# Chunk choice for both head groups at once, two blocks in halves, and loads reordered, in a fused attention and feed-forward kernel

## The chip, the cores and the metric

The kernel runs on one core of one Trainium2 chip. The metric is the device time of one execution in microseconds (us), as a median over runs. The engines are named as in the profile: PE is TensorE (matmuls), PEld its weight loads, DVE is VectorE, ACT is ScalarE, POOL is GpSimd and SP is SyncE, which here only starts DMAs. Every instruction of the profile carries the kernel line that issued it, such as L834.

## The reference

Two parts follow one another. The first is attention with a choice of key chunks: 4 batches, 8 heads, 768 tokens, 64 dimensions, keys in chunks of 32.

```python
k_min, k_max = min and max of k over each chunk of 32 keys
ub = sum_d(max(q * k_min, q * k_max))           # one bound for each query and chunk
ub = where(chunk is not in the future, ub, -1e9)
sel = the 6 chunks of highest ub for each query
scores = where(sel & causal, q @ k.T / 8, -1e9)
attn_out = softmax(scores) @ v
```

The second takes the result as 3072 tokens of width 512, normalizes by the root mean square (times `rms_g`), and computes `(silu(x @ w_gate) * (x @ w_val)) @ w_out` with an inner width of 1536. Inputs and output are float32; inside the kernel most tensors are bf16.

## The kernel before

The work is cut into 12 blocks of 256 tokens (4 batches, 3 blocks m = 0, 1, 2 of each). `ORDER` lists them; blocks 0 to 3 of the order are the first blocks (m = 0) of the four batches. Each block has two head groups of four heads, and each pair of block and group is one call of `job`. Within it:

- `turn` transposes k and q on DVE (L525), `half` makes bf16 copies (L532, L533), `ext0` and `ext1` take minimum and maximum of each chunk (L540), and `dk`, `bd0`, `bd1` put them into the matrix BD (L545, L552).
- `upper` (L587) multiplies q and its positive part with BD on PE: 32 small matmuls, the bounds of all chunks. For m = 0 only the last 64 columns of each head pair need them, since earlier tokens have at most six chunks.
- `ubn` (L597) transposes the bounds on DVE, `bar` (L604) sets the future chunk to a large negative value, `top` (L611) finds the eight largest, `mk` (L616) compares with the sixth, `mt` (L620) and `swap` (L627 on DVE or L631, L632 on ACT) turn the mask for use on PE as mtd and mto.
- `scores` (L657, and L668 for the mask) goes into the PSUM buffers S, `exp` (L707, ACT) into pt, the triangle (L677, POOL) clears the future, `values` (L733, PE) multiplies with v, and `rden` and `norm` (L748, L752) divide.

`norm` turns a block's tokens into xsT (L768 to L809, with PE transposes L796). `ffn` runs the gate and value matmuls wg and wv (L834, called gates here) into the PSUM buffers F, tanh (L841, ACT), tg (L845, DVE), a copy vs (L853, ACT) and the product hh (L856, POOL), or, where `DIRECT` says so, the product on DVE straight from PSUM (L849). `project` (L866) multiplies hh with wo, `out` copies (L880, L882), and SP stores (L886).

Block 0 is in `SPLIT`: its tokens go in two halves of 128, its first half needs no mask, and its gates have 128 moving columns instead of 256. A gate step of 512 columns (two or four of wo's 128 rows) needs one third of wg and wv: the weights come in three DMAs each, wg, wv in turns and then wo, all issued by POOL. The inputs are issued by SP and, for block 0, by ACT.

Nothing is ordered by hand: `Plan` simulates the engines with assumed durations, gives each operation a priority, and writes out the order in which the engines get their instructions. `pool` holds numbered buffers; pools named in `in_order`, hh among them, are given out strictly in the order of the program. `due_attn` and `due_ffn` place a block's attention 70 us ahead of its feed-forward part. Where PE would idle before 60 us, the planner puts in matmuls of the identity with itself (`keep_busy`, L921): filler that computes nothing that is used. `HELD` makes the loads of two blocks wait for a weight:

```python
HELD = {2: (("wv", 2), ("wo", 1)), 3: (("wo", 1), ("wo", 2))}   # block: (before k and q, before v)
```

S has 2 buffers (a scores step takes both, an upper step one), F has 4, hh 13, pt 6.

Of the kernel before, what the change touches and what calls it, by code (L numbers as in the profile page):

```python
# [8 lines left out]
FP32 = mybir.dt.float32  # L9
# [8 lines left out]
NEG = -1.0e30  # L18
# [3 lines left out]
class Op:  # L22
# [3 lines left out]
    def __init__(self, name, eng, occ, lat, fn, pri):  # L26
        self.name, self.eng, self.occ, self.lat, self.fn, self.pri = name, eng, occ, lat, fn, pri
        self.deps, self.takes, self.uses, self.users, self.after = [], [], [], [], []
        self.dma = None
        self.slack = 0.0  # L30
        self.mode = None
        self.done = None
        self.alts = {eng: (occ, lat, fn)}


class Rings:

# [6 lines left out]
    def _step(self, until):  # L44
        while True:
            heads = [q[0] for q in self.queue.values() if q]
            nxt = self.wait[0][0] if self.wait else None
            if not heads:
                if nxt is None or nxt > until:
                    return  # L50
                self.now = max(self.now, nxt)
            else:
                cycle = sum(d[1] for d in heads)
                end = self.now + min(d[0] for d in heads) * cycle
                stop = min(end, until, nxt if nxt is not None else end)
                if stop > self.now:
                    for d in heads:
                        d[0] -= (stop - self.now) / cycle
                    self.now = stop
                for q in self.queue.values():  # L60
                    if q and q[0][0] <= 1e-9:
                        q[0][2](self.now)
                        q.pop(0)
            while self.wait and self.wait[0][0] <= self.now + 1e-12:
                _, ring, d = self.wait.pop(0)
                self.queue.setdefault(ring, []).append(d)
            if self.now >= until and not (self.wait and self.wait[0][0] <= until):
                if not any(q and q[0][0] <= 1e-9 for q in self.queue.values()):
                    return

    def add(self, t, ring, packets, cost, op):
        self._step(min(t, self.wait[0][0]) if self.wait else t)

        def landed(now, op=op):
            op.done = now + (0.9 if op.dma[2] else 1.2) + op.slack
        op.done = None
        self.wait.append((t, ring, [packets, cost, landed]))
        self.wait.sort(key=lambda w: w[0])
        self.guess()
# [28 lines left out]
class Plan:  # L108
# [4 lines left out]
    PATIENT = {}  # L113
# [38 lines left out]
    def run(self, in_order=(), fill=None):  # L152
# [25 lines left out]
        def est(o, e):  # L178
# [6 lines left out]
            for key in o.takes:  # L185
                p = self.pool_of[key]
                need[p] = need.get(p, 0) + 1
                if p in strict and self.fifo[p][head[p]] is not o:
                    return None
# [18 lines left out]
        while todo:  # L208
# [58 lines left out]
            for key in o.takes:  # L267
                p = self.pool_of[key]
                if p in strict:
                    head[p] += 1  # L270
                self.free[p].sort()
                slot[key] = self.free[p].pop(0)[1]
# [16 lines left out]
def kernel(  # L289
# [37 lines left out]
    def buffers(name, n, shape, dtype, space=sb):  # L327
        store[name] = [space.tile(shape, dtype, name=f"{name}{i}") for i in range(n)]
        plan.pool(name, n)
# [13 lines left out]
    buffers("ubn", 2, [P, 2, 4, CH], FP32)  # L343
    buffers("m8", 2, [P, 2, 4, 8], FP32)
    buffers("mk", 2, [P, 2, 4, CH], BF16)
    buffers("mtd", 5, [P, 2, 4, CH], BF16)
    buffers("mto", 5, [P, 4, CH], BF16)
# [34 lines left out]
    PACE, LEAD = 23.0, 70.0  # L382
    MARGIN = 3.0
    FIRST = 8
    SPLIT = {0}
    PACKED = {0, 1, 2}
    DIRECT = {(i, hp) for i in range(len(ORDER)) for hp in range(KH) if i >= 6 and hp % 2}
# [67 lines left out]
    HELD = {2: (("wv", 2), ("wo", 1)), 3: (("wo", 1), ("wo", 2))}  # L455

    def load_qk(i, nm, src):
# [3 lines left out]
        for n, a in enumerate((0, 2, 1, 3)):  # L461
            eng = ("SP", "ACT")[n % 2] if i == 0 else "SP"
            rows = slice(32 * a, 32 * (a + 1))
            if i in PACKED:
                sv = src[b].rearrange("(g a) (m r j) d -> a m r g (j d)", a=4, m=NBLK, r=32)[a, m]
                todo = [(sv, lambda rows=rows: at(key)[rows].rearrange("r g j h d -> r g (j h d)"),
                         4, 0.098)]
# [14 lines left out]
    def loads_due(i, n):  # L482
        return -500 + 10 * i + n if i < 2 else due_attn(i) - 30 + n

    def load_v(i):
        b, m = ORDER[i]
        key = ("vraw", b, m)
        for e in range(2):
# [3 lines left out]
                64, 0.02, loads_due(i, 2 if i != 1 else -1), writes=[key],  # L492
# [14 lines left out]


    def job(i, g):
# [67 lines left out]
        ub, ubn, m8, mk = ("ub", *J), ("ubn", *J), ("m8", *J), ("mk", *J)  # L577
        mtd, mto = ("mtd", *J), ("mto", *J)

        def upper():  # L580
            qs = [at(qT)[:, :, BLK - w:], qr()]
            qs = [x.rearrange("p h (j c r) -> p h j c r", c=2, r=CH) for x in qs]
            o, d = at(ub), BD[b, g]
            for t in range(4):
                for hp in range(2):
                    for c in range(2):
                        TE.matmul(o[64 * c:64 * (c + 1), hp, 0:32 * nj],  # L587
                                  d[64 * hp:64 * (hp + 1), t, :],
                                  qs[t // 2][64 * hp:64 * (hp + 1), t % 2, :, c, :],
                                  start=(t == 0), stop=(t == 3))  # L590

        o = plan.op(f"upper{J}", "PE", 0.925 if m else 0.49, 1.09 if m else 0.66, upper, base + 3,
                    reads=[bd] + [bd + (x,) for x in range(m + 1)] + [qT, qR, qraw], writes=[ub],
                    takes=[(ub, "S")])
        o.mode = "sq"
        j0 = 4 - nj
        plan.op(f"ubn{J}", "DVE", 0.37 if m else 0.17, 0.445 if m else 0.25, lambda: VE.transpose(  # L597
            out=at(ubn).rearrange("p h j c -> p h (j c)")[:, :, 0:32 * nj],
            in_=at(ub)[:, :, 0:32 * nj]), base + 3, reads=[ub], writes=[ubn], takes=[(ubn, "ubn")])

        def bar():
            f = at(ubn)[0:64].rearrange("p h j c -> p h (j c)")
            c = CB * m + 2 * j0 + 1
            VE.memset(f[:, :, c:c + 34 * (nj - 1) + 1:34], NEG)  # L604

        plan.op(f"bar{J}", "DVE", 0.09, 0.12, bar, base + 3, reads=[ubn], writes=[ubn])

        def top():
            for h in range(2):
                for j in range(nj):  # L610
                    VE.max(out=at(m8)[:, h, j, :],  # L611
                           in_=at(ubn)[:, h, j, 0:CB * m + 2 * (j0 + j) + 2])

        plan.op(f"top{J}", "DVE", 0.083 * 2 * nj, 0.083 * 2 * nj + 0.08, top, base + 3,
                reads=[ubn], writes=[m8], takes=[(m8, "m8")])
        plan.op(f"mk{J}", "DVE", 0.35 if m else 0.15, 0.42 if m else 0.22, lambda: VE.tensor_tensor(  # L616
            out=at(mk)[:, :, 0:nj], in0=at(ubn)[:, :, 0:nj],
            in1=at(m8)[:, :, 0:nj, TOPK - 1:TOPK].to_broadcast([P, 2, nj, CH]), op=ALU.is_lt),
            base + 3, reads=[ubn, m8], writes=[mk], takes=[(mk, "mk")])
        plan.op(f"mt{J}", "DVE", 0.37 if m else 0.17, 0.445 if m else 0.245, lambda: VE.transpose(  # L620
            out=at(mtd).rearrange("p h j c -> p h (j c)")[:, :, 0:32 * nj],
            in_=at(mk).rearrange("p h j c -> p h (j c)")[:, :, 0:32 * nj]),
            base + 3, reads=[mk], writes=[mtd], takes=[(mtd, "mtd")])

        def swap():
            for r, c, h in ((slice(0, 64), slice(64, 128), 0), (slice(64, 128), slice(0, 64), 1)):
                VE.transpose(out=at(mto)[r].rearrange("p j c -> p (j c)")[:, 0:32 * nj],  # L627
                             in_=at(mk)[c, h].rearrange("p j c -> p (j c)")[:, 0:32 * nj])

        def swap_act():  # L630
            SE.activation(out=at(mto)[0:64, 0:nj], in_=at(mtd)[64:128, 0, 0:nj], func=ACT.Copy)  # L631
            SE.activation(out=at(mto)[64:128, 0:nj], in_=at(mtd)[0:64, 1, 0:nj], func=ACT.Copy)  # L632

        flex(f"swap{J}", {"DVE": (0.42 if m else 0.28, 0.5 if m else 0.36, swap), "ACT": (0.65, 0.66, swap_act)}, base + 3,
             reads=[mtd, mk], writes=[mto], takes=[(mto, "mto")])
# [10 lines left out]
        def unit(kg, sc, tiles, masked):  # L646
# [3 lines left out]
            for e, q0, q1, c0 in tiles:  # L650
# [9 lines left out]
                for d in range(2) if mask else ():  # L660
                    for a in range(4):
# [5 lines left out]
                        mv = (at(mtd)[r, hp] if d == 0 else at(mto)[r])[:, jq - j0:nj, :]  # L667
# [13 lines left out]
        for kg in [m] + list(range(m)):  # L681
# [11 lines left out]
            for part, tiles, c0, c1, pe, occ, lat in parts:  # L693
# [7 lines left out]
                            reads=[("kb", *jk), qb] + ([mtd, mto, "chunkrow"] if masked else []),  # L701
# [20 lines left out]
        for s in range(2):  # L722
# [14 lines left out]
            pri = base + (-4 if i in SPLIT and not s else 6)  # L737
# [78 lines left out]
    def ffn(i, toks):  # L816
# [7 lines left out]
        for hp in range(KH):  # L824
# [4 lines left out]
            for nm, p_, w in (("wg", gp, wg), ("wv", vp, wv)):  # L829
# [12 lines left out]
                out=at(th), in_=at(gp), func=ACT.Tanh, scale=0.5), pri, reads=[gp], writes=[th],  # L842
# [16 lines left out]
        for k_, s in enumerate(toks):  # L859
# [3 lines left out]
            def project(h0, h1, k_=k_, op=op):  # L863
                for ht in range(h0, h1):
# [11 lines left out]
                        lambda project=project: project(last, NHT), pri - 20,  # L876
# [7 lines left out]
                pri, reads=[op], writes=[ob], takes=[(ob, "osb")])  # L884
# [15 lines left out]
    for i in range(len(ORDER)):  # L900
        if i > 1:
            loads(i)
        for g in range(NG):
            job(i, g)
# [50 lines left out]
```

## Time and profile before

| | us |
|---|---|
| median of 5 runs | 308.58 |
| lowest and highest | 308.44, 309.35 |
| the profiled execution | 309.29 |
| its span, first to last instruction | 307.5 |
| DVE busy / ACT busy / POOL busy | 218.0 / 218.0 / 150.8 |

The granted TensorE clock was 0.997 over the span. 30.65 MB were moved; until about 45 us the DMA engines are full, and after 180 us nearly idle. Busy shares are means over stretches with different limits, so the stretches have to be looked at one by one. A row of the groups gives busy time and mean duration, then the idle time of the engine before these instructions and what ended it. PE's instructions are pipelined: a matmul's duration is longer than its distance from the next one, and costs on PE are read from start to start.

### The profile page before, as it was taken

The numbers are of one execution on the slowest core, as the hardware profiler recorded it, in microseconds if no ns is written. First come the engines' busy times: TensorE is split into PE (matmuls) and PEld (weight loads), VectorE is DVE, ScalarE is ACT, GpSimd is POOL, SyncE is SP. The second block draws the span as 40 slices with busy tenths as digits, with TensorE's granted clock in tenths as the row PEclk, the third lists the DMA queues.
The fourth block names the chain that finished last, engine by engine and source line by source line (L and its number), as shares of the span: only waits on it lengthen the run. The fifth ranks groups of instructions, "written<-read, shape, count | busy, mean of one in ns | idle before, by whom it ended". The sixth has DMA issues, their size and how long they took to land.

```text
span 307.5 us, 11834 instructions
## 1 busy us (share of the span) xinstructions
PE 295.4 (96%) x4899; PEld 229.1 (74%) x4899; DVE 218.0 (71%) x606; ACT 218.0 (71%) x386; POOL 150.8 (49%) x272
## 2 busy tenths in 40 slices
PE   8897899999999999999999999999999999999994
PEld 8696895866867866885887787688588598688671
DVE  7895588887898999889589688268478145247250
ACT  3675696967776997997698877678578379565240
POOL 4794384956683674766478544164033134114130
PEclk9999999999999999999999999999999999999998
DMA  8999995775754722754565300100010010110101
GB/s 195 238 215 208 235 196 134 143 204 114 199 133 128 162 44 70 171 117 95 155 149 130 105 4 3 68 5 2 11 61 3 2 71 2 36 36 0 70 0 68
DMA packets 74838, 30.65 MB, mean 100 GB/s; under 512 B 65569, under 2 KB 70177, under 8 KB 74785
## 3 DMA queue, kind: packets, MB, share of 16 engines
q1 hardware_dynamic: 69184, 24.66, 32.6%
q0 software_dynamic: 4752, 4.72, 9.3%
q8 instruction: 38, 0.62, 0.9%
q10 hardware_dynamic: 848, 0.53, 0.6%
q14 instruction: 16, 0.12, 0.1%
HBM read 28.31 MB, written 6.29 MB: 113 GB/s over the span
## 4 chain that ended last, share of the span: by engine, by line
PE 88%; ACT 3%; POOL 2%; DVE 2%; issue 2%; DMA 2%; ACTq 0%; DVEq 0%; POOLq 0%
PE F L834 40%; PE F L866 21%; PE S L657 7%; PE F L733 7%; PE S L587 6%; PE S L668 3%; PE F L921 2%; PE F L796 2%; DMA qraw<-in_q_dram 2%; POOL pt L677 1%; ACT th L841 1%; DVE qT L525 1%; ACT pt L707 1%; ACT vs L853 1%; ACT junk L768 0%
## 5 line engine op out<-in xcount | busy, mean ns | idle before, releaser
L707 ACT ACTIVATE pt<-S 128x1024 bf16<-128x1024 f32 (+3 forms) x100 | 86.0, 890 | 24.3 <-PE S L668 23.4
L856 POOL TENSOR_TENSOR hh<-tg,vs 128x512 bf16<-128x512 bf16 x54 | 62.3, 1156 | 71.7 <-ACT vs L853 31.6
L834 PE MATMUL F<-xsT,wg 128*128 128x256 bf16 (+1 forms) x624 | 74.9, 265 | 0.2 <-DVE xnat L752 0.2
L834 PE MATMUL F<-xsT,wv 128*128 128x256 bf16 (+1 forms) x624 | 74.9, 265 | 0.0
L845 DVE SCALAR_TENSOR_TENSOR tg<-th,F 128x512 bf16<-128x512 bf16 x72 | 48.9, 679 | 33.2 <-ACT th L841 32.5
L866 PE MATMUL F<-wo,hh 128*128 128x512 bf16 x288 | 67.2, 380 | 0.0
L834 PEld LDWEIGHTS <-wg 128*128 128x128 bf16 x624 | 55.6, 98 | 9.3 <-issue 1.6
L834 PEld LDWEIGHTS <-wv 128*128 128x128 bf16 x624 | 55.7, 98 | 7.4 <-issue 0.3
L841 ACT ACTIVATE th<-F 128x512 bf16<-128x512 f32 x72 | 43.3, 601 | 14.7 <-PE F L834 12.9
L866 PEld LDWEIGHTS <-hh 128*128 128x128 bf16 x288 | 26.3, 98 | 28.6 <-issue 0.2
L677 POOL TENSOR_SCALAR_AFFINE_SELECT pt<-pt 128x512 bf16<-128x512 bf16 x48 | 30.6, 642 | 26.0 <-ACT pt L707 24.7
L853 ACT ACTIVATE vs<-F 128x512 bf16<-128x512 f32 x54 | 32.5, 601 | 6.3 <-PE F L834 5.9
L657 PE MATMUL S<-qb,kb 32*128 32x256 bf16 (+1 forms) x784 | 32.4, 255 | 0.8 <-ACT qb L532 0.7
L540 DVE TENSOR_REDUCE kx<-kT 128x16 f32<-128x512 f32 x48 | 29.8, 664 | 0.0
L733 PE MATMUL F<-VX,pt 128*128 128x65 bf16 x672 | 26.3, 194 | 1.8 <-POOL hh L856 1.2
L733 PEld LDWEIGHTS <-pt 128*128 128x128 bf16 x672 | 24.0, 98 | 3.7 <-POOL hh L856 1.3
L882 DVE TENSOR_SCALAR osb<-F 128x512 f32<-128x512 f32 x14 | 9.4, 686 | 19.5 <-PE F L866 19.3
L657 PEld LDWEIGHTS <-kb 32*128 32x128 bf16 x784 | 13.4, 92 | 13.0 <-issue 11.9
L768 ACT ACTIVATE junk<-xnat 128x512 bf16<-128x512 bf16 x24 | 15.1, 629 | 10.5 <-DVE xnat L752 10.1
L921 PE MATMUL F<-ident 128*128 128x128 bf16 x275 | 19.6, 232 | 2.1 <-POOL ident masks.py:199 1.4
L668 PE MATMUL S<-mtd,chunkrow 32*128 32x128 bf16 (+2 forms) x384 | 20.3, 203 | 0.0
L668 PE MATMUL S<-mto,chunkrow 32*128 32x128 bf16 (+2 forms) x384 | 20.0, 203 | 0.0
(60 smaller groups left out, 374.1 us busy)
## 6 DMA issues: line engine op xcount, KB each, us to landing
vraw<-in_v_dram SPq DMA_DIRECT2D x24, 256.0 KB, 4.3
out_dram<-osb SPq DMA_DIRECT2D x24, 256.0 KB, 2.1
kraw<-in_k_dram SPq DMA_DIRECT2D x72, 64.0 KB, 2.7
qraw<-in_q_dram SPq DMA_DIRECT2D x72, 64.0 KB, 2.1
wg<-in_moe_w_gate_dram POOLq DMA_DIRECT2D x3, 512.0 KB, 10.8
wv<-in_moe_w_val_dram POOLq DMA_DIRECT2D x3, 512.0 KB, 12.5
wo<-in_moe_w_out_dram POOLq DMA_DIRECT2D x3, 512.0 KB, 19.1
kraw<-in_k_dram SPq DMA_DIRECT2D x10, 128.0 KB, 5.1
```

Of the source, the lines that this page charges most:

```text
L540: plan.op(f"ext{n}{J}", "DVE", 0.585, 0.67, lambda n=n, op=op: VE.tensor_reduce(out=at(kx)[:, n], in_=at(kT).rearrange("p h (c t) -> p h c ...
L657: TE.matmul(s[a // 2][:, a % 2, c0:c0 + q1 - q0], kbt[r, t, ks], qbt[r, t, q0:q1], start=(t == 0), stop=(t == 1 and not mask), skip_group_ ...
L668: TE.matmul(o, chunkrow[r, BLK * kg + P * e:BLK * kg + P * (e + 1)], mv, start=False, stop=(d == 1), skip_group_check=True)
L677: GE.affine_select(out=d, in_=d, compare_op=ALU.is_ge, fill=0.0, base=0, pattern=[[0, 4], [1, P]], channel_multiplier=-1)
L707: lambda pt=pt, hs=hs, c0=c0, c1=c1, x=sc[hp]: SE.activation(out=at(pt)[:, hs, c0:c1], in_=at(x)[:, :, c0:c1], func=ACT.Exp, scale=SCALE), ...
L733: TE.matmul(o[:, a, :], p_[:, a, off:off + P], vt[:, e, a, :], start=(kb_ == 0 and a == 0), stop=(kb_ == nkb - 1 and a == 3), skip_group_c ...
L834: TE.matmul(at(p_)[:, n * W:(n + 1) * W], w[:, g, ht * P:(ht + 1) * P], at(xT)[:, g, 0:W], start=(g == 0), stop=(g == NP - 1), skip_group_ ...
L841: plan.op(f"tanh{U}.{hp}", "ACT", 0.48, 0.6, lambda th=th, gp=gp: SE.activation(out=at(th), in_=at(gp), func=ACT.Tanh, scale=0.5), pri, re ...
L845: VE.scalar_tensor_tensor(out=at(tg), in0=at(th), scalar=1.0, in1=at(gp), op0=ALU.add, op1=ALU.mult), pri - 30, reads=[th, gp], writes=[tg ...
L853: plan.op(f"vcopy{U}.{hp}", "ACT", 0.48, 0.6, lambda vs=vs, vp=vp: SE.activation(out=at(vs), in_=at(vp), func=ACT.Copy), pri + 0.1, reads= ...
L856: plan.op(f"hh{U}.{hp}", "POOL", 1.11, 1.16, lambda tg=tg, vs=vs, hh=hh: GE.tensor_tensor(out=at(hh), in0=at(tg), in1=at(vs), op=ALU.mult) ...
L866: TE.matmul(at(op)[:], at(("hh", *U, ht // K))[:, o:o + P], wo[:, ht, :], start=(ht == 0), stop=(ht == NHT - 1))
```

## The change

`pick` takes the bounds, the choice and the mask out of `job` and does them for both head groups of a block in single operations: one upper step with both groups' matmuls into one S buffer, then one transpose, one memset, the same number of max8, one comparison and one transpose of the mask, over twice the columns; the swap likewise. `SPLIT` takes in block 1. `HELD` lets block 2's k and q follow the first third of wg, its v the first of wv, and block 3's loads the first third of wo. Block 1's v is queued after its q. hh buffers may be given out of order, as long as those ahead in the line still find one (`RESERVED`). `DIRECT` starts at block 4 instead of 6. In the planner, DVE may wait up to 0.3 us for a more urgent operation (`PATIENT`), DMAs start later behind queued weights (`FETCHED`), and some costs and priorities change.

```diff
+    FETCHED = 3.3
...
+                ahead = sum(x[0] * x[1] for x in self.queue.get("POOL", ()))
+                if ring != "POOL" and not d[3] and ahead > 0.0 and not self.queue.get(ring):
+                    d[3] = True
+                    self.wait.append((self.now + min(self.FETCHED, ahead), ring, d))
...
-    PATIENT = {}
+    PATIENT = {"DVE": 0.3}
+    RESERVED = ("hh",)
...
+                    if line[h] is not o:
+                        if p not in self.RESERVED:
+                            return None
+                        before = sum(x.start is None for x in line[h:line.index(o)])
+                        if len(self.free[p]) <= before:
+                            return None
...
-    buffers("ubn", 2, [P, 2, 4, CH], FP32)
+    buffers("ubn", 1, [P, NG, 2, 4, CH], FP32)
...
-    buffers("mtd", 5, [P, 2, 4, CH], BF16)
-    buffers("mto", 5, [P, 4, CH], BF16)
+    buffers("mtd", 3, [P, NG, 2, 4, CH], BF16)
+    buffers("mto", 3, [P, NG, 4, CH], BF16)
...
-    SPLIT = {0}
+    SPLIT = {0, 1}
+    APART = set()
...
-    DIRECT = {(i, hp) for i in range(len(ORDER)) for hp in range(KH) if i >= 6 and hp % 2}
+    DIRECT = {(i, hp) for i in range(len(ORDER)) for hp in range(KH) if i >= 4 and hp % 2}
...
-    HELD = {2: (("wv", 2), ("wo", 1)), 3: (("wo", 1), ("wo", 2))}
+    HELD = {2: (("wg", 0), ("wv", 0)), 3: (("wo", 0), ("wo", 0))}
...
-                64, 0.02, loads_due(i, 2 if i != 1 else -1), writes=[key],
+                64, 0.023 if i < 2 else 0.019, loads_due(i, 2), writes=[key],
...
+    def pick(i, gs):
...
+        def bank():
+            return at(ub)[:, :, 0:n * 32 * nj].rearrange("p h (g n) -> p g h n", g=n)
...
+            for k_, g in enumerate(gs):
...
+                for t in range(4):
+                    for hp in range(2):
+                        for c in range(2):
+                            TE.matmul(bank()[64 * c:64 * (c + 1), k_, hp],
+                                      d[64 * hp:64 * (hp + 1), t, :],
+                                      qs[t // 2][64 * hp:64 * (hp + 1), t % 2, :, c, :],
...
+        plan.op(f"ubn{tag}", "DVE", turned, turned + 0.08, lambda: VE.transpose(out=flat(ubn), in_=bank()),
...
+            for g in gs:
+                for h in range(2):
+                    for j in range(nj):
+                        VE.max(out=at(m8)[:, g, h, j, :],
+                               in_=at(ubn)[:, g, h, j, 0:CB * m + 2 * (j0 + j) + 2])
...
-            pri = base + (-4 if i in SPLIT and not s else 6)
+            pri = base + (-4 if i in SPLIT and not s else 9)
...
-                out=at(th), in_=at(gp), func=ACT.Tanh, scale=0.5), pri, reads=[gp], writes=[th],
+                out=at(th), in_=at(gp), func=ACT.Tanh, scale=0.5), pri - 20, reads=[gp], writes=[th],
...
-                        lambda project=project: project(last, NHT), pri - 20,
+                        lambda project=project: project(last, NHT), pri - 10,
...
-        for g in range(NG):
-            job(i, g)
+        jobs = [job(i, g) for g in range(NG)]
...
+            for j in jobs:
+                next(j)
+            pick(i, tuple(range(NG)))
+            for j in jobs:
+                next(j, None)
```

## The prediction

> **What bounds the kernel now.** I read the page first, then a table of busy time by stretch, PE's waits, PE's timeline and the groups by shape.
>
> ```profile
> PE 295.4 (96%) x4899; PEld 229.1 (74%) x4899; DVE 218.0 (71%) x606; ACT 218.0 (71%) x386; POOL 150.8 (49%) x272
> ```
>
> PE is busy 96% of the span. Part of that is filler (L921, 275 matmuls of 56 ns start to start, 15.4 us), all before 64 us. From 80 us to the last matmul at 303 us I find only about 1 us between PE's matmuls that switching between forms does not explain. So there is nothing to win after 80 us except PE work itself, and anything that makes PE wait there is lost. The start is another matter. Busy time by stretch, cut at PE's stalls (columns: length, then busy us and count of PE, PEld, DVE, ACT, POOL, then clock, DMA share, GB/s):
>
> ```profile
> 14.70:20.66 5.96, 5.88 (x128) 5.57 (x128) 5.27 (x14) 4.36 (x11) 5.35 (x11) 1.00 1.23 218
> 20.68:26.80 6.12, 3.98 (x126) 3.59 (x126) 4.09 (x13) 3.90 (x9) 5.03 (x12) 1.00 1.24 208
> 26.82:32.70 5.88, 4.73 (x128) 4.22 (x128) 3.83 (x13) 3.71 (x6) 2.57 (x4) 1.00 1.24 206
> ```
>
> Between two stalls PE issues 128 matmuls and 128 weight loads, 256 instructions, three times over, each time in about 6.0 us. The stalls have no releaser, or one that does not fit:
>
> ```profile
> PE S L587 <- issue: 2.2, 1, 2.2
> PE F L733 <- POOL hh L856: 1.2, 1, 1.2
> ```
> ```profile
> 24.41 0.28 PE L587 MATMUL S<-qraw,BD 64*64 64x32 f32 x3
> 26.84 0.42 PE L587 MATMUL S<-qraw,BD 64*64 64x32 f32 x13 [2.15 <-issue]
> ```
>
> The first stops PE after 3 of 16 matmuls that wait for nothing new; the second is put down to an hh product that values (L733) do not read. The packet records of the page's queue "q8 instruction: 38 packets, 0.62 MB" (9798 matmuls and weight loads in 38 packets are 258 each) settle it: a packet starts at 24.36 and at 30.44, 3.6 to 3.7 us after PE entered the block before, and PE goes on 2.3 to 2.5 us after the packet's start. While the weights fill the DMA engines (10.6 to 42.5 us), 256 PE instructions cost at least 6 us. I count 2.36 + 1.32 us lost at the two stalls, start to start.
>
> The other loss is filler between real work: 18 matmuls at 24 to 31 us (1.2 us), 32 at 41.14 (1.8 us), while block 1's turned input is missing, and 8 at 63.3 (1.1 us). Waits of 0.2 to 0.7 us at 71.4, 73.6, 74.8 and 112.4 add 1.6.
>
> ```profile
> 40.69 0.61 PE L796 MATMUL F<-ident,xs 128*128 128x128 bf16 x8
> 41.14 1.95 PE L921 MATMUL F<-ident 128*128 128x128 bf16 x32
> 42.92 1.04 PE L834 MATMUL F<-xsT,wg 128*128 128x256 bf16 x8
> ```
>
> **Merged choice (pick).** PE: the matmuls of upper (L587) stay; a run of both groups together takes 1.91 us to the next line's start (77, 154.8, 204.3 us), two single runs 2 x 1.04, and each run's entry costs 0.09. So a merge saves 2.26 - 2.00 = 0.26 us, and 1.40 - 1.16 = 0.24 for the 32-column form. Five later blocks and two first ones are apart now: 7 x 0.25 = -1.8 us, all on the path. DVE:
>
> ```profile
> L616 DVE TENSOR_TENSOR mk<-ubn,m 128x256 bf16<-128x256 f32 x16 | 6.8, 428 | 0.1
> L616 DVE TENSOR_TENSOR mk<-ubn,m 128x64 bf16<-128x64 f32 x8 | 2.1, 276 | 0.0
> ```
>
> Per element (428 - 276)/192 = 0.79 ns, so 512 elements take about 631 against 2 x 428 = 856: -0.22 us a block. The same from ubn (444, 240) and mt (427, 226) gives -0.17 and -0.16, bar -0.06, swap about -0.2: -0.8 a later block. The max8 stay at 144. DVE is not on the path; counted zero there. The first group's mask comes about 1.5 us later (eight more max8 of 0.09, longer transposes); gates (L834) of earlier blocks hide it, and without them it costs that 1.5 once per block. Upper holds an S buffer of two once for about 2.9 us instead of twice for about 1.7: zero.
>
> **Halves of block 1.** 192 gate matmuls of 128 columns at 56 ns replace 96 of 256 at 109: +0.3 us. Two more score groups enter and leave the row form, 0.25 each: +0.5. Extra exps, one rms and xsT lie on ACT and POOL beside PE. Block 1's first half needs no mask, so its gates no longer wait for the whole block.
>
> **Loads and hh order.** SP waits 19.4 us for wv's last third before block 2's loads:
>
> ```profile
> SPq L402 <- DMA wv<-in_moe_w_val_dram: 19.4, 1, 19.4
> ```
>
> After, k and q of block 2 follow the first wg (landed 19.13), v the first wv (21.67), block 3 the first wo. Each weight now lands 2.5 to 2.6 us after the one before; beside block 2's k and q the last two took 4.04 and 4.07, so k and q cost 3.0 us of DMA and v, by its landings at 44.1 and 44.8 after q's at 42.9, some 1.7. All 4.7 can go ahead of four weights: wv's last third then lands at 36.5 instead of 31.8 (it is used at 34.05 today). RESERVED covers this: hh buffers may be taken out of order, so PE can run two thirds of four halves, 8 x 1.8 = 14.4 us of gates, before the last thirds. Without that cover, up to 2.5 us. Block 1's k and q go ahead of its v on SP, so k lands about 2.7 us earlier (v's two landings took 1.2 and 1.6); v is then queued last, and the values at 23.6 need it at the earliest.
>
> **Sum of the front.** From 20.7 us the gates of blocks 0 and 1 and block 1's attention are: before, done at 42.92 plus 96 x 0.109 = 53.4. After, execution alone: 384 gate matmuls (21.5), block 1's attention 3.6 (upper 1.16, scores 2 x 0.63, values 24 x 0.033, turn 0.45), the two extra score groups 0.5, the rest of block 0's attention 0.9, so 47.2. By instructions, matmuls and weight loads: 2 x 384 gates, 352 attention, 88 left of block 0, 1208 = 4.7 blocks of 256 at 6.04 = 28.5 us, so 49.2. The gain is between 6.2 and 4.2. I take the latter, since the weights keep the engines full to about 46, less 1.2 for thirds and inputs that are not there yet (today's filler at 24 to 31): -3.0. The bounds are -6.2 and, if block 2's attention is drawn into the loaded stretch, about zero.
>
> [...]
>
> **DIRECT and priorities.** Six hh products of blocks 4 and 5 go to DVE, 6 x 0.683 = +4.1 us, and six copies leave ACT (-3.6) and six products POOL (-6.9). That falls between 92 and 138 us:
>
> ```profile
> 92.00:138.00 46.00, 45.71 (x828) 35.62 (x827) 42.33 (x137) 40.42 (x72) 27.70 (x48) 1.00 0.48 115
> ```
>
> DVE is at 42.3 of 46. Three merges give 2.4 back: 44.0, still under 46, so zero; with the cover gone 1.7. PATIENT may idle DVE up to 0.3 us at a time; unknown, 0 to 4 us there. The new priorities only reorder; bounds -2.7 (the small waits after 60 us gone) to +2, taken zero. The tail (last project, copy, store from 298 us) keeps its instructions.
>
> Total against the profiled execution's 309.29 (span 307.5 and 1.8 around it): -3.0 - 1.8 + 0.8 = -4.0, 305.3. That execution lay 0.7 above the median 308.58, so the forecast is 304.6.
>
> **Rivals.** (a) *The stalls only move.* Block 2's attention, 320 instructions, enters the loaded stretch: 1.25 blocks at 6.04 = 7.5 us against 3.9 of execution before, so 49.2 + 7.5 + 1.2 = 57.9 against 53.4 + 3.9 = 57.3. The front gives +0.6, the merges net -1.0: about 308.2. For it: two of three stretches above already run at the limit. Against: each gate-only block of 256 takes 7.2 us, over the limit.
> (b) *VectorE becomes the bound between 92 and 138 us.* 42.3 + 4.1 + 4 of PATIENT's idling = 50.4 in 46, and merged choices that wait for both groups return nothing: +4.4, against -1.5 at the front and -1.0 net of merging: 308.58 + 1.9 = 310.5. It decides once DVE passes 46 there. For it: 92% busy today. Against: ACT and POOL are relieved, and attention runs blocks ahead of its gates.
>
> **Numbers.** A difference of about 0.2% (0.6 us) is what a measurement here can tell. Forecast 304.6: 0.53 (by itself 301 to 307.5). Rival (a) 308.2: 0.22. Rival (b) 310.5: 0.25. Faster: 0.52 + 0.10 + 0.01 = 0.63; same: 0.01 + 0.07 + 0.01 = 0.09; slower 0.05 + 0.23 = 0.28. The range runs from 300.5 (front at its bound, -6.2, net merging -1.0, a third of the later waits, -0.9) to 310.8 (rival b, with 0.3 for the spread of single runs).
>
> **What would show it.** Right: block 1's gates in 128 columns start before 35 us, filler after 21 us under 1 us, L587 in 12 runs, PE free of waits from 80 us. Stalls at every 256th PE instruction should remain while weights land. Wrong: PE waits on DVE tg or hh past 90 us, or gates that wait for wg or wv near 36 us.

## The result, and the profile after

The changed kernel takes 308.19 us (median of 31 runs, 306.95 to 309.25), the kernel before 308.73 (52 runs). The ratio is 0.9983, 95% interval 0.9976 to 0.9990: 0.5 us faster, where 4.0 were forecast. The profiled execution took 307.88 us, its span 306.2, at a granted clock of 0.998. First the page's row of PE:

```profile
PE 293.6 (96%) x4992; PEld 229.9 (75%) x4992; DVE 218.5 (71%) x560; ACT 210.4 (69%) x364; POOL 146.4 (48%) x266
```

PE issues 93 more matmuls than before in 1.8 us less busy time; DVE has 46 instructions fewer and no less work. PE's waits:

```profile
PE S L559 <- issue: 1.8, 1, 1.8
PE F L793 <- issue: 1.4, 1, 1.4
PE F L894 <- issue: 0.8, 1, 0.8
```

There are now three large stalls without a releaser where before had two (one of those booked to hh). They stand behind PE's instructions 960, 1216 and 1472 (952, 1208 and 1464 matmuls and weight loads and 8 semaphore instructions), each time 256 apart, at whatever line PE happens to be (upper L559, values L793, gates L894). The two stalls of before stand at 960 and 1216 by the same count. In PE's timeline (start, length, then what ran, and the idle time before it):

```profile
24.18 0.31 PE L559 MATMUL S<-qT,BD 64*64 64x32 f32 x6
26.27 0.32 PE L559 MATMUL S<-qT,BD 64*64 64x32 f32 x8 [1.77 <-issue]
...
28.08 1.57 PE L991 MATMUL F<-ident 128*128 128x128 bf16 x25
29.50 0.40 PE L856 MATMUL F<-ident,xs 128*128 128x128 bf16 x4
...
32.74 0.30 PE L793 MATMUL F<-VX,pt 128*128 128x65 bf16 x4 [1.37 <-issue]
32.88 1.05 PE L894 MATMUL F<-xsT,wg 128*128 128x128 bf16 x16
...
39.21 0.40 PE L894 MATMUL F<-xsT,wg 128*128 128x128 bf16 x4 [0.79 <-issue]
```

PE goes on at 26.27, 32.74 and 39.21: 6.47 us for each of the two blocks of 256 instructions between. Between the stalls, cut at them (length, then busy us and count of PE, PEld, DVE, ACT, POOL, clock, DMA share, GB/s):

```profile
26.25:31.20 4.95, 4.93 (x128) 4.54 (x128) 2.52 (x11) 3.02 (x9) 1.53 (x3) 1.00 1.19 237
32.70:38.20 5.50, 5.46 (x127) 5.32 (x128) 4.54 (x10) 4.23 (x10) 3.20 (x6) 1.00 1.22 197
```

PE runs its 256 instructions in 4.95 and 5.5 us and then stands until the 6.47 are over. Part of those instructions computes nothing. PE's groups from 20.69 us to the end of the stall at 32.72, and the filler of before in the same stretch:

```profile
L991 PE MATMUL F<-ident 128*128 128x128 bf16 x52 | 3.7, 220 | 0.0
L894 PE MATMUL F<-xsT,wv 128*128 128x128 bf16 x32 | 2.1, 220 | 0.0
...
L894 PE MATMUL F<-xsT,wg 128*128 128x128 bf16 x16 | 1.1, 219 | 0.0
```
```profile
L921 PE MATMUL F<-ident 128*128 128x128 bf16 x18 | 1.5, 220 | 0.0
```

L991 is the filler (L921 before): 52 matmuls, where before had 18. From the start to 32.72 us it is 252 against 235, and with the 16 gates (L894) of the time before, both kernels have issued exactly 64 gate matmuls by then. The halves have gained nothing so far.

The other lines that answer to those of before: SP now waits for the first wg and the first wo, no longer for wv's last third, and wv's last third lands at 36.45 us (31.84 before).

```profile
SPq L419 <- DMA wo<-in_moe_w_out_dram: 13.0, 1, 13.0
SPq L419 <- DMA wg<-in_moe_w_gate_dram: 7.8, 1, 7.8
```

The mask's comparison does both groups at once, and the stretch in which DVE was nearest to its limit has room left (DVE 42.33 before, PE 45.71):

```profile
L600 DVE TENSOR_TENSOR mk<-ubn,m 128x512 bf16<-128x512 f32 x8 | 5.5, 694 | 0.1
L600 DVE TENSOR_TENSOR mk<-ubn,m 128x128 bf16<-128x128 f32 x4 | 1.2, 292 | 0.1
```
```profile
92.00:138.00 46.00, 46.00 (x833) 35.70 (x835) 40.75 (x126) 35.48 (x60) 26.15 (x43) 1.00 0.47 114
```

How far the changed kernel is ahead when both have done the same PE work (filler left out; my own account from the two traces): -1.7 us at 38 us (behind), 0.3 at 60, 1.35 at 65 (the 8 fillers at 63 us are gone), 1.8 at 75, 2.0 at 140, 1.5 at the end. These two executions lie 1.4 us apart, the medians 0.5; the difference is the spread of single runs.

### The profile page after: what moved, and what is told of

Its sections match the earlier page's. It is cut to its first block, busy times and chain, and to the rows that moved or that the text cites. A ratio compares the mean times of both kernels' runs of the same rounds, so it can differ in the third digit from the quotient of the medians.

```text
span 306.2 us, 11929 instructions
## 1 busy us (share of the span) xinstructions
PE 293.6 (96%) x4992; PEld 229.9 (75%) x4992; DVE 218.5 (71%) x560; ACT 210.4 (69%) x364; POOL 146.4 (48%) x266
## 4 chain that ended last, share of the span: by engine, by line
PE 87%; DMA 4%; DVE 3%; issue 2%; ACT 1%; ACTq 0%; POOL 0%; DVEq 0%
PE F L894 40%; PE F L926 21%; PE S L717 7%; PE F L793 7%; PE S L559 6%; PE S L728 3%; DMA wg<-in_moe_w_gate_dram 3%; PE F L856 2%; DMA qraw<-in_q_dram 2%; PE F L991 1%; DVE kx L654 1%; DVE qT L639 1%; DVE tg L905 1%; ACT junk L828 0%; ACT th L901 0%
## 5 line engine op out<-in xcount | busy, mean ns | idle before, releaser
L916 POOL TENSOR_TENSOR hh<-tg,vs 128x512 bf16<-128x512 bf16 x48 | 55.8, 1167 | 66.4 <-ACT vs L913 44.3
L894 PE MATMUL F<-xsT,wg 128*128 128x256 bf16 (+1 forms) x672 | 75.0, 258 | 1.3 <-issue 0.8
L894 PE MATMUL F<-xsT,wv 128*128 128x256 bf16 (+1 forms) x672 | 74.7, 258 | 0.0
L894 PEld LDWEIGHTS <-wg 128*128 128x128 bf16 x672 | 56.5, 98 | 9.3 <-issue 1.8
L894 PEld LDWEIGHTS <-wv 128*128 128x128 bf16 x672 | 57.2, 98 | 7.5 <-issue 0.3
L901 ACT ACTIVATE th<-F 128x512 bf16<-128x512 f32 x72 | 43.0, 598 | 20.7 <-PE F L894 17.8
L913 ACT ACTIVATE vs<-F 128x512 bf16<-128x512 f32 x48 | 28.4, 600 | 9.3 <-PE F L894 8.4
L793 PE MATMUL F<-VX,pt 128*128 128x65 bf16 x672 | 27.1, 194 | 2.2 <-issue 1.4
L793 PEld LDWEIGHTS <-pt 128*128 128x128 bf16 x672 | 24.0, 98 | 4.5 <-issue 2.9
L812 DVE TENSOR_TENSOR xnat<-F,rden 128x256 bf16<-128x256 f32 x48 | 20.1, 423 | 1.3
L991 PE MATMUL F<-ident 128*128 128x128 bf16 x256 | 18.1, 231 | 1.6 <-POOL ident masks.py:199 1.4
```

Source lines behind the costliest of these rows:

```text
L793: TE.matmul(o[:, a, :], p_[:, a, off:off + P], vt[:, e, a, :], start=(kb_ == 0 and a == 0), stop=(kb_ == nkb - 1 and a == 3), skip_group_c ...
L894: TE.matmul(at(p_)[:, n * W:(n + 1) * W], w[:, g, ht * P:(ht + 1) * P], at(xT)[:, g, 0:W], start=(g == 0), stop=(g == NP - 1), skip_group_ ...
L901: plan.op(f"tanh{U}.{hp}", "ACT", 0.48, 0.6, lambda th=th, gp=gp: SE.activation(out=at(th), in_=at(gp), func=ACT.Tanh, scale=0.5), pri - 2 ...
L913: plan.op(f"vcopy{U}.{hp}", "ACT", 0.48, 0.6, lambda vs=vs, vp=vp: SE.activation(out=at(vs), in_=at(vp), func=ACT.Copy), pri + 0.1, reads= ...
L916: plan.op(f"hh{U}.{hp}", "POOL", 1.11, 1.16, lambda tg=tg, vs=vs, hh=hh: GE.tensor_tensor(out=at(hh), in0=at(tg), in1=at(vs), op=ALU.mult) ...
```

## The experiments

Below, (C) is the theory that code blocks limit the front; against it stand theories by which PE lacks work (weights, inputs or attention that are not there: W, S), and the clock (G). All ratios are against the kernel before, with 95% intervals; all kernels but the two marked "before" start from the changed one.

### Parts taken out or done alone

**Merge undone.**

```diff
-    APART = set()
+    APART = set(range(12))
```

> The changed kernel, but with the bounds, choice and mask of each head group on its own again (APART holds all blocks). If the merge is worth what the form changes on PE say, seven merges of 0.25 us (in fact twelve, if the planner keeps all groups apart: up to 3.0 us) are lost and the time is 309.8 to 311.2. If PE's waits elsewhere swallow the merge, the time stays at 308.2 within 0.4.

310.49 us, 1.0052 (1.0033 to 1.0070): the merged choice is worth 2.3 us. Upper is entered in 20 runs instead of 12; at the prediction's 0.25 us that is 2.0. Five of the six runs had a clock of 0.999 or 1.000; the profiled one had a stretch of low clock after a wait:

```profile
19.08 0.17 PE L728 MATMUL S<-mto,chunkrow 32*128 32x32 bf16 x1
21.25 0.19 PE L728 MATMUL S<-mto,chunkrow 32*128 32x32 bf16 x3 [2.00 <-issue]
```
```profile
18.00:24.00 6.00, 4.00 (x80) 3.46 (x77) 3.03 (x7) 3.51 (x7) 4.07 (x7) 0.79 1.22 218
```

**Old loads.**

```diff
-    HELD = {2: (("wg", 0), ("wv", 0)), 3: (("wo", 0), ("wo", 0))}
+    HELD = {2: (("wv", 2), ("wo", 1)), 3: (("wo", 1), ("wo", 2))}
```

> The changed kernel, but block 2's and 3's loads wait for the weights as before (HELD of the kernel before). Theory W (the loads drawn ahead of the weights starve the gates and eat the front's gain): the last third of wv lands at 32 us instead of 36.5, filler after 20 us falls from 54 matmuls to under 20 and the time falls by 1.5 to 3 us, to 305.2 to 306.7. Theory C (code blocks of 256 PE instructions bound the start whatever the loads do): stalls of 1 to 2.4 us at every 256th PE instruction remain, and the time changes by less than 0.5 us.

312.70, 1.0128 (1.0110 to 1.0146). The front itself became faster than the changed kernel's (1.4 us ahead of before at 60 us, 2.4 at 65). All of it and more went from 67 to 79 us: PE waited for masks and inputs of later blocks, and the clock fell to half:

```profile
70.00:80.00 10.00, 7.79 (x90) 5.96 (x91) 8.07 (x19) 7.29 (x14) 6.99 (x15) 0.66 0.61 142
```

So early weights were paid for with late inputs of blocks 2 and 3, and the early inputs are worth more. A setting between the two is tried below.

**Early loads alone, on the kernel before.**

```diff
-    HELD = {2: (("wv", 2), ("wo", 1)), 3: (("wo", 1), ("wo", 2))}
+    HELD = {2: (("wg", 0), ("wv", 0)), 3: (("wo", 0), ("wo", 0))}
```

> The kernel before with the changed kernel's HELD alone: block 2's loads go ahead of four weights. Theory W on its own (weights are late by up to 4.6 us, and the kernel before has no gates of other halves to run meanwhile): slower by 1 to 3 us, 309.7 to 311.7. If early loads help by earlier attention at 66 to 80 us, faster by 0.5 to 2 us.

312.85, 1.0132 (1.0116 to 1.0148): 4.1 us lost. Its profile has waits of 1.17 us at 20.5, 0.97 at 38 and 1.79 at 43.5, 117 filler matmuls after 20 us where before has 58, and half clock for 3.41 us from 23.30. Without the rest of the change the delayed weights are not covered; that the halves are what covers them was not tested alone.

**Block 1 whole.**

```diff
-    SPLIT = {0, 1}
+    SPLIT = {0}
```

> The changed kernel with only block 0 in halves. 192 gate instructions and some 32 of the scores fall away before 48 us. Theory C: that is 0.9 of a code block of 6 us less, and the time falls by 1 to 3 us. Theory W: block 1's first half no longer gives early gates while weights are late, and the time rises by 1 to 3 us.

312.53, 1.0117 (1.0099 to 1.0134). Fewer instructions at the front, and 4.3 us slower all the same: the theory that halves only cost instructions fails here. The loss is larger than a lack of work at the front alone was said to give; a stall of 2.5 us, a wait of 1.7 us at 111.7 and a stretch of half clock behind it (3.41 us at 113.9) are in its profile.

**DIRECT from block 6, no PATIENT, old priorities.** Three kernels with one edit each:

```diff
-    DIRECT = {(i, hp) for i in range(len(ORDER)) for hp in range(KH) if i >= 4 and hp % 2}
+    DIRECT = {(i, hp) for i in range(len(ORDER)) for hp in range(KH) if i >= 6 and hp % 2}
```
```diff
-    PATIENT = {"DVE": 0.3}
+    PATIENT = {}
```
```diff
-            pri = base + (-4 if i in SPLIT and not s else 9)
+            pri = base + (-4 if i in SPLIT and not s else 6)
...
-                in_=at(gp), func=ACT.Tanh, scale=0.5), pri - 20, reads=[gp], writes=[th],
+                in_=at(gp), func=ACT.Tanh, scale=0.5), pri, reads=[gp], writes=[th],
...
-                        lambda project=project: project(last, NHT), pri - 10,
+                        lambda project=project: project(last, NHT), pri - 20,
```

> The changed kernel with DIRECT from block 6 as before: six hh products go back from VectorE to GpSimd, with six copies on ScalarE. If VectorE at 92 to 138 us costs the change something, the time falls by 0.7 us or more; if the load on VectorE is hidden, it stays within 0.6 us.

> The changed kernel without PATIENT. The prediction gave it 0 to 4 us of idling on VectorE at 92 to 138 us. If that idling is on the path, the time falls by 0.7 to 3 us; if hidden, it stays within 0.6 us; if waiting for urgent work helps, it rises.

> The changed kernel with the three old priorities (values 6, tanh as its gates, last project step 20 ahead). The prediction took them as zero. If they only reorder, within 0.6 us of 308.2; if they cost the change its gain, 305.5 to 307.5; if they are part of it, above 309.

309.74, 1.0024 (1.0010 to 1.0037); 310.07, 1.0047 (1.0029 to 1.0066); 310.59, 1.0056 (1.0043 to 1.0070). Each of the three edits, taken as zero by the prediction, costs 1.5 to 2.4 us. For the two last the profiles show waits that the changed kernel has not: without PATIENT 1.6 us before 39.61 us (transposes that wait for ScalarE) and 0.5 and 0.6 at 135; with the old priorities 0.9 at 41.5 and 1.8 at 114. For DIRECT they show none. Up to 45 us PE's order is the changed kernel's, but PE enters a block of code at 20.74 us instead of 20.16, behind a stall of 0.9 us that the changed kernel has not; PE is then 0.8 us late at 67 us and at its last matmul alike, and it is busy 46.00 of the 46 us from 92 to 138 in both kernels. Behind the last matmul the profiled execution takes 1.1 us longer. So what the six products on DVE are worth stays open.

Taken out one at a time, the parts are worth 2.3, 4.5, 4.3, 1.5, 1.9 and 2.4 us, 16.9 together; all of them in bring 0.5. They lean on one another: each of these six edits lets the planner write a new order, and an edit made alone on the kernel before (the loads) costs 4.1. The order of hh, block 1's loads and `FETCHED` were not undone.

### The filler's instructions

**Filler only until 20 us.**

```diff
-                      fill=(1.6, 5.6, 60.0, 0.0565, "F", keep_busy)):
+                      fill=(1.6, 5.6, 20.0, 0.0565, "F", keep_busy)):
```

> The changed kernel without filler after 20 us (54 filler matmuls with their weight loads, 108 PE instructions, left out; they compute nothing that is used). Theory C: the code blocks last longer in real work, the stalls after 20 us (1.99, 1.53, 0.95 us) shrink by 1.5 to 2.5 us together, and the time falls by 1 to 2 us. Theory W: PE only waits where it filled, and the time stays within 0.4 us.

309.15, 1.0003 (0.9986 to 1.0020): inconclusive. One stall of 2.45 us is left, and PE's work is 1.5 us ahead at 60 us, but the clock is at half for 6.83 us from 25.38:

```profile
20.00:30.00 10.00, 7.20 (x154) 6.12 (x145) 6.04 (x23) 4.99 (x14) 5.17 (x11) 0.77 1.18 248
```

Saved instructions and lost clock can't be told apart here, so the next kernels keep PE as long at work with fewer or more instructions. Wide and narrow filler change what is written out for a run of filler and nothing that the planner sees: in their traces all other PE instructions come in the changed kernel's order.

**Wide filler.** After the first run, four filler matmuls of 128 columns become one of 512, of the same length.

```diff
     def keep_busy(n, slot):
-        for _ in range(n):
+        calls.append(n)
+        wide = n // 4 if len(calls) > 1 else 0
+        for _ in range(wide):
+            TE.matmul(store["F"][slot][:, 0:512], ident[:], chunkrow[:, 0:512], start=True, stop=True)
+        for _ in range(n - 4 * wide):
             TE.matmul(store["F"][slot][:, 0:P], ident[:], ident[:], start=True, stop=True)
```

> The changed kernel with the same filler time in a quarter of the instructions: after the first run of filler, each four filler matmuls of 128 columns become one of 512 (filler computes nothing that is used). Some 120 matmuls with their weight loads, 250 PE instructions, leave the stretch before 48 us. Theory C (code blocks of 256 PE instructions, 6 us each while the weights land, bound the start): one block less, the stalls after 20 us (4.5 us together) fall by 2 us or more, and the time falls by 1 to 3 us, to 305.2 to 307.2. Theory S (the supply of work bounds: turned inputs, weights and, from 66 to 80 us, the attention of later blocks): PE gets its work no earlier, the gain is handed back by 80 us, and the time stays within 0.6 us.

306.32, 0.9920 (0.9904 to 0.9936): 1.9 us faster than the changed kernel, with the same computation and 240 PE instructions fewer. In PE's timeline the stalls on code shrink to 0.6 us, and a weight is waited for instead:

```profile
29.91 0.45 PE L894 MATMUL F<-xsT,wv 128*128 128x128 bf16 x5 [0.94 <-DMA wv<-in_moe_w_val_dram]
30.97 0.79 PE L894 MATMUL F<-xsT,wv 128*128 128x128 bf16 x11 [0.60 <-issue]
...
37.44 0.73 PE L894 MATMUL F<-xsT,wg 128*128 128x128 bf16 x10 [0.63 <-issue]
```

From 30.97 to 37.44 it is 6.47 us again.

**Narrow filler.** The same time of filler in twice the instructions.

```diff
-        for _ in range(n):
+        if len(calls) > 1:
+            for _ in range(2 * n):
+                TE.matmul(store["F"][slot][:, 0:64], ident[:], ident[:, 0:64], start=True, stop=True)
+            return
+        for _ in range(n):
```

> The changed kernel with the same filler time in twice the instructions: after the first run, each filler matmul of 128 columns becomes two of 64 (filler computes nothing that is used). Some 170 matmuls with their weight loads, 340 PE instructions, are added before 48 us, which is 1.3 code blocks. Theory C: the time rises by 1.5 to 5 us, to 309.7 to 313. Theory S: within 0.6 us of 308.2.

316.22, 1.0252 (1.0231 to 1.0273): 8.0 us slower than the changed kernel, more than was expected. The page has 5162 matmuls, 340 PE instructions more. At 6.04 us for 256, the prediction's price, these are 340/256 x 6.04 = 8.0 us; at 6.47, 8.6. PE's timeline where it goes on, and two stretches between stalls:

```profile
19.86 0.42 PE L995 MATMUL F<-ident 128*128 128x64 bf16 x9 [2.95 <-issue]
...
26.06 0.21 PE L717 MATMUL S<-qb,kb 32*128 32x128 bf16 x1 [2.45 <-issue]
...
32.43 0.31 PE L559 MATMUL S<-qraw,BD 64*64 64x32 f32 x1 [2.29 <-issue]
...
45.37 0.51 PE L894 MATMUL F<-xsT,wg 128*128 128x128 bf16 x6 [1.40 <-issue]
```
```profile
13.30:16.70 3.40, 3.40 (x126) 3.36 (x127) 2.47 (x13) 1.28 (x4) 2.79 (x6) 1.00 1.30 213
26.10:29.90 3.80, 3.80 (x124) 3.51 (x126) 2.88 (x10) 2.77 (x7) 1.43 (x5) 1.00 1.18 260
```

PE runs 250 to 253 recorded instructions in 3.4 and 3.8 us and then stands for 2.3 to 3 us, until 6.2 to 6.6 us are over: how short the block's work is does not matter. From 32.43 to 45.37 two blocks take 12.94 us, with no stall between them; the clock was at 0.66 between 30 and 40 us, which cost at most what these two blocks take over 2 x 6.04, 0.9 us. This settles C as what the filler costs.

**Wide filler on the kernel before.** The edit is the same.

> The kernel before with the same wide filler. Theory C: the stalls of 2.36 and 1.32 us shrink and the time falls by 1 to 2.5 us. Theory S: within 0.6 us.

308.85, 1.0000 (0.9984 to 1.0017). The code stalls go here too (0.42 us left at 33.7), but from 40.28 us gates of block 1 wait for a tg (L845), and DVE comes to that only behind a transposition of block 2's k, which lands at 41.09 us:

```profile
PE F L834 <- DVE tg L845: 2.2, 1, 2.2
```
```profile
41.12 1.10 DVE L525 STREAM_TRANSPOSE kT<-kraw 128x512 f32<-128x512 f32 x1 [4.60 <-DMA kraw<-in_k_dram]
42.07 0.67 DVE L845 SCALAR_TENSOR_TENSOR tg<-th,F 128x512 bf16<-128x512 bf16 x1
```

The kernel before has the same order on DVE here, and there this transposition begins at 40.67, with k's landing at 40.65:

```profile
40.67 1.12 DVE L525 STREAM_TRANSPOSE kT<-kraw 128x512 f32<-128x512 f32 x1 [0.41 <-DMA kraw<-in_k_dram]
```

So the front of before is tied to block 2's k, whose load waits for wv's last third, whatever the code costs: S holds there. Fewer filler instructions are worth something only with the rest of the change; whether the halves or the early loads are what they need was not taken apart.

**Wide filler, old loads, filler until 95 us.** The edits of the two kernels above, and 95.0 in place of 60.0.

> The changed kernel with the loads of blocks 2 and 3 held as before, wide filler, and filler allowed to 95 us instead of 60, so that PE keeps its clock at the waits of 67 to 79 us. Held loads alone took 312.7 us, with the clock at half for 3.4 us at 27 us and for 6.8 us at 72 us. Theory G (the clock gate is the loss): without the two low stretches, worth 5.1 us at most, the time is 307.5 to 309.5. Theory S: PE still waits for the attention of blocks 3 and 4 at 67 to 79 us, the waits turn into filler, and the time stays above 310.5.

312.80, 1.0130 (1.0101 to 1.0160). The front is 3.5 us ahead at 60 us and 4.5 at 65, the clock stays at 1.00 from 64 to 80 us, and at 80 us everything is lost. PE's waits, and its busy time from 64 to 80 us:

```profile
PE F L856 <- ACT osb L940: 1.6, 1, 1.6
...
PE S L728 <- DVE mtd L604: 1.2, 1, 1.2
```
```profile
64.00:80.00 16.00, 11.23 (x173) 8.26 (x170) 14.05 (x39) 10.99 (x22) 8.62 (x19) 1.00 0.73 183
```

The changed kernel has PE busy for 14.83 of the same 16 us and DVE for 10.13. Here DVE still has attention to do (14.05), and PE waits for ACT and for DVE's masks. What late inputs of blocks 2 and 3 cost is supply (S), not the clock (G).

**Wide filler, two weights ahead of block 2.** Block 2's k and q follow the second wg, its v the second wv.

```diff
-    HELD = {2: (("wg", 0), ("wv", 0)), 3: (("wo", 0), ("wo", 0))}
+    HELD = {2: (("wg", 1), ("wv", 1)), 3: (("wo", 0), ("wo", 0))}
```

> The changed kernel with wide filler, and block 2's k, q and v one third of the weights later (behind the second wg and wv). Theory W: the second and third parts of the weights land up to 4 us earlier, and the time falls by 0.5 to 2 us below the 306.3 of wide filler alone. Theory S (block 2 to 4's attention is what PE lacks at 66 to 80 us, and its loads must come early): the front gains and hands it back, or more: 306 to 309.

305.12 (304.46 to 305.85), 0.9875 (0.9855 to 0.9895): 3.6 us faster than before, 3.1 than the changed kernel, the lowest median of all. PE's order is still the changed kernel's. The last wv lands at 34.71 us instead of 36.45, and no gate waits for a weight. In the chain that ended last, of the changed kernel and of this one, the two long runs of gates behind block 1's halves:

```profile
40.09 4.47 PE F L894 x80
...
44.78 4.47 PE F L894 x80
```
```profile
37.19 4.47 PE F L894 x80
...
41.88 4.47 PE F L894 x80
```

The front is 2.9 us earlier than the changed kernel's, very nearly the gain that the prediction had given it over before.

**The same loads with the old filler.**

> The changed kernel with its own narrow filler, and block 2's loads behind the second wg and wv. Theory W alone: the weights land earlier whatever the filler, and the time falls by 1 to 2 us, to 306.2 to 307.2. Theory C first: PE goes on at the pace of its code blocks, the earlier weights find no gates issued, and the time stays within 0.6 us of 308.2.

307.94, 0.9972 (0.9957 to 0.9987; 11 runs): 0.25 us under the changed kernel, which the two intervals (0.9976 to 0.9990 there) do not tell from nothing. With a quarter of the filler's instructions the same loads bring 306.32 - 305.12 = 1.2. So code comes first and the weights behind it.

**The first run of filler wide, too.** It starts before `ident` is there, on a tile of ones (256 columns), with the loads of the changed kernel and with those of the fastest.

```diff
+        k, lhs, rhs = (2, ones256[:, 0:P], ones256) if first else (4, ident[:], chunkrow)
```

> The changed kernel with wide filler from the start: the first run of 86 filler matmuls becomes 43 of 256 columns as well, 86 PE instructions less before 8 us (filler computes nothing that is used). Theory C: a third of a code block, up to 2 us, more room before 40 us: 304.5 to 306.3. If PE by then waits for weights and inputs, 306.3 within 0.5.

> Both: wide filler from the start, and block 2's loads one third of the weights later. If code blocks and weights each hold the front back, this is the fastest: 304 to 306. If the supply at 66 to 80 us binds, no faster than the wide filler alone: 306 to 309.

305.70, 0.9902 (0.9887 to 0.9918), and 305.25, 0.9889 (0.9870 to 0.9908). The first is 0.6 us under the kernel with only the later filler wide, with intervals that overlap; the second is no better than 305.12. So a gain from the first run's instructions is not shown.

## Why the prediction was wrong in size

**The front, -3.0: the step that failed.** The working priced 1208 instructions from 20.7 us at 6.04 us for 256, and added 1.2 us for thirds and inputs that are not there; gates of blocks 0 and 1 were to end at 49.2 + 1.2 = 50.4. In the trace the 19th of their 24 runs of 16 begins at 48.19; with 0.90 for each of the six left they would end at 53.6 (work of block 2 comes between), 3.2 us later, level with the 53.4 of before. Two terms were mis-sized, the 1.2 for holes and the flat 6.04.

The 1.2: block 0's second half was assumed to feed gates when its first half was done; its turn comes at 29.50 us and its first gate at 32.88, and block 1's gates begin at 39.93 at the earliest, not before 35. Into these holes the planner put 56 filler matmuls after 20 us, 112 instructions. At 6.04 us for 256 they cost 2.6 us of code, and only 1.2 was allowed.

The flat 6.04: up to 39.21 us PE was given 704 instructions in 18.5 us, where 6.04 for 256 gives 16.6. The 520 behind, nearly all gates, take 14.4 where it gives 12.3: 16 gates take 0.90 us, so 256 instructions of gates take 7.2 and are bound by execution, not by code. The prediction names the 7.2 against rival (a), but its sum takes the larger of two totals (26.5 us of execution, 28.5 of code), where each block takes the larger of its own two.

By luck a third error hid part of this: 96 of the 1208 instructions (a run of gates and attention of block 0) were done before 20.7 us, worth 2.3. So 1.4 for filler, 1.9 and 2.1 for the price, less 2.3, make 3.1 of the 3.2 us. The narrow and the wide filler show by experiment that filler's code costs; the two terms of the price are read from the trace alone. Why a block takes 6.47 us here and took 5.9 to 6.1 before was not found out. The packet records show where it goes: the packet of the next block starts 4.06 and 4.17 us after PE enters the two blocks of 6.47 us, against the 3.6 to 3.7 of before.

**The stalls** were right: they stay at every 256th instruction while weights land, and I had the price of a block within 7%. The error was to apply it to the work that is used and not to everything PE is given, and to blocks of gates that last longer by themselves. Start to start, the stalls at these instructions took 0.3 to 3.1 us.

**The merge, -1.8 on PE,** was right as far as the runs show: upper is entered in 12 runs (19 before), a merged run still takes 1.91 us, and undoing it costs 2.3. On DVE the comparison takes 694 ns for 512 elements, estimated 631; DVE is not on the path.

**The loads.** wv's last third was forecast for 36.5 us and landed at 36.45, and no gate waited for it in the changed kernel. What covered it was in part filler and stalls; when the wide filler takes these away, 1.6 us of waits for wv appear, within the "up to 2.5" of the prediction.

**DIRECT, PATIENT and priorities** were set to zero; undoing each costs 1.5 to 2.4 us. That PE would be free of waits past 80 us was right but for 0.6 us at 177.6 and 0.3 at 180.8. Without PATIENT and with the old priorities there are more and longer waits, which a sum by durations does not show; for DIRECT the profile shows no such wait.

**Rival (a)** named 308.2, and the time is 308.19, but not by its mechanism: block 2's upper begins at 49.18 us, behind the loaded stretch. That the stalls only move was its right half; what filled the blocks was filler. **Rival (b)** is refuted: DVE has 40.75 us of 46 between 92 and 138, PE 46.00, and with DIRECT back at block 6 the kernel is slower, not faster.

**What stays open:** what DIRECT is worth, why the block's price differs, and what limits the fastest kernel now.

## What to carry to other kernels

While weights fill the DMA engines, count the instructions of a stretch as well as its time, and give each block of 256 the larger of its execution and the time that a block with a stall takes (here 5.9 to 6.6 us, save for 5.1 and 6.9 in two runs). Small filler matmuls paid for their code here: 340 PE instructions more in the same filler time cost 8.0 us, and 240 fewer, in wide matmuls, saved 1.9, so filler should be few wide ones. Before a gain is booked at a front, list when each input becomes usable, for a hole there is filled with something that has a price of its own (here 2.6 us of code for 56 filler matmuls, by the estimate above). Parts of a change that are planned together can't be priced by undoing them one by one: here they add to 16.9 us, and together bring 0.5.

## What the runs showed of the hardware

- Under full DMA engines a block of 256 PE instructions that ended in a stall took 5.9 to 6.6 us before, after and with narrow filler, often 6.47, with 3.4 us of execution in it as with 5.5 (5.1 us with the first run of filler wide, 6.9 with the merge undone); twice the filler instructions in the same filler time cost 8.0 us, a quarter of them saved 1.9. By the packet records the next packet of the instruction queue (39 packets and 0.64 MB in the changed kernel) started 3.6 to 4.2 us after PE entered a block in the first three (2.6 and 4.5 in the other two), and PE went on 2.3 to 2.5 us after that start in all. With the weights landed, the changed kernel's packet started 0.4 us after the entry at 46.13 us, and the next block was entered at 50.82 without a stall.
- A wait of PE of 2.00 us was followed by half clock for 3.41 us with the merge undone (0.79 between 18 and 24 us); with filler until 20 us, which has a stall of 2.45 us, the clock was at half for 6.83 us. Other waits were not followed by it: before and after have waits of 2.15 and 1.77 us at clocks of 0.997 and 0.998 over the span, and the narrow filler's wait of 2.95 us before 19.86 was followed by full clock (1.00 from 19.83 to 26.05).
- Block 2's first load of k landed 4.8 us after its issue (19.00 to 23.82) while weights were landing, its other loads of k and q after 6.7 to 8.1 us; held for one weight more, the first took 5.9 us (23.91 to 29.84). Over the whole kernel the median for k is 2.6 us.
